# Twelve matmuls ahead of all else, decay rows padded to 128, thirty more fills and a new order in a fused mixer kernel

## The chip, the cores and the metric

The kernel runs as one program on one core of a Trainium2 chip. The metric is the device time of one execution in microseconds (us), as the median of the runs. A profile holds one execution; its span goes from the first to the last instruction. Engines are named as the profile names them: PE (TensorE matmuls), PEld (its weight loads), DVE (VectorE), ACT (ScalarE), POOL (GpSimd), SP (SyncE, which issues most DMAs).

## What is computed

Three layers follow one another, for 4 batches, 8 heads, 768 steps and head size 40 (model width 320):

```python
def _attn_ref(q, k, v, i_gate, f_gate, o_gate):
    ...
    for t in range(S):
        m_new = np.maximum(f_gate[:, :, t] + m, i_gate[:, :, t])
        f_stab = np.exp(f_gate[:, :, t] + m - m_new)
        i_stab = np.exp(i_gate[:, :, t] - m_new)
        m = m_new
        C = f_stab[:, :, None, None] * C + i_stab[:, :, None, None] * np.einsum('bhd,bhe->bhde', vt, kt)
        n = f_stab[:, :, None] * n + i_stab[:, :, None] * kt
        ...
        y[:, :, t] = o * h_tilde / denom

def _moe_ref(x, w_val, conv_w, w_out):      # causal convolution of 5 taps as a gate
    ...
    val = x @ w_val
    return (gate * val @ w_out).astype(np.float32)

def _moe2_ref(x, w_ch1, w_ch2):             # Fourier mixing, layer norm, two-layer perceptron
    X = np.fft.fft(np.fft.fft(x, axis=1), axis=2)
    u = x + np.real(X).astype(np.float32)
    ...
    ch = np.maximum(un @ w_ch1, 0.0) @ w_ch2
    return (u + ch).astype(np.float32)
```

## The kernel before

**Attention.** The recurrence is cut into chunks of 128 steps, six for each batch, and each chunk into two halves of 64 steps. For a chunk the decay of each head is spread over 128 partitions by matmuls into a PSUM bank (`a_fb`), and DVE scans that bank into `d` (`a_pre`). For the first four chunks of batch 0 `a_fb` uses 16 small matmuls of 32 rows (the profile's `bank<-f,pat`). For all 20 other chunks it is one matmul of 24 rows and 512 columns, `bank<-gsp,sel`: `gsp` holds the decay rows of the four batches, 24 rows for each, at partitions 0, 32, 64 and 96 of one buffer; `sel` is a constant that picks rows. Then come `bank<-qk` (40 rows), `bank<-kvo` and `bank<-kvo,d` (64 rows, 41 columns), `bank<-cc,e` (40 rows) and, for batch 0, `bank<-eg,epat` (32 rows). None of these uses all 128 rows of the array. Each float32 matmul of the program stands in the profile as two instructions.

**Gate and mixing.** The output of a chunk is transposed (`bank<-pat,x`), three chunks make a half of a batch, and on it run the convolution (`xT,dg` on PE for three of the pieces, DVE for the rest), the value product (`xH,wvH` and seven like it), the output product (`woH,gH` and so on), the Fourier steps (`cs,eo`, `dmat,w`), a layer norm and the perceptron (`uu,w1H` ... and `w2H,hh` ...). These use all 128 rows. The weights come as 64-bit floats, are taken apart by DVE and ACT (`raw` to `mk`) and split into high and low parts.

**What sets the order.** Every operation is recorded as a unit in a list (`_Plan`), and `emit` replays the units in the order of the table `ORDER`, written out by hand or by a search outside the kernel; `CELL` says which buffer or PSUM bank each tile gets. So every engine's queue is fixed by `ORDER`. The table `FILLS` inserts extra matmuls before a unit: `(n, m, k)` puts m products of a constant 128x128 tile into bank k before unit n; nobody reads their result. In the profile they are `bank<-pat` of L343, and there are 42. All recorded instructions have one line, L292, so that tile names tell them apart.

The steps that the change touches are `fill` (L341 to L344), `prologue_pads` (L389), `prologue_spread` (L436), which loads `gsp` once for all batches, `prologue_const` (L450), which loads `sel`, `a_fb` (L577), and the replay `emit` (L279). The first operations on PE are two transposes of the input gate, which wait for the constant `pat`.

Of the kernel before, what the change touches and what calls it, by code (L numbers as in the profile page):

```python
# [33 lines left out]
NQK = 2  # L34
FB0 = 4
# [131 lines left out]
]  # L167
FILLS = [
    (25, 1, 3), (207, 4, 6), (199, 5, 6), (219, 2, 4), (426, 2, 1), (460, 2, 0), (488, 4, 1), (515, 15, 3), (575, 5,
    3), (1023, 2, 1),  # L170
]

# [83 lines left out]
class _Plan:  # L256
# [7 lines left out]
    def add(self, eng, method, a, k):  # L264
# [9 lines left out]
        for x in sorted(ins, key=lambda x: x.t is out):  # L274
            if not x.t.n:
                self.tiles.append(x.t)
                x.t.n = len(self.tiles)

    def emit(self):  # L279
        held = [t for t in self.tiles if t.kind is not None]  # L280
        for t, n in zip(held, CELL, strict=True):
            t.cell = n
# [896 lines left out]
```

## Time and profile before

| | us |
|---|---|
| median of 3 runs (502.08 to 503.85) | 502.46 |
| the profiled execution, its own time | 502.64 |
| its span | 500.8 |
| PE busy in the span | 470.4 (94%) |
| PEld busy | 428.5 (86%) |
| DVE busy | 336.9 (67%) |
| ACT busy | 179.2 (36%) |
| POOL busy | 152.7 (30%) |

Around the span lie 1.84 us. In the chain of work that ended last PE has 69% and DVE 17%. The rows are read so: a row of the timeline has the start in us from the start of the span, the length of the group, the engine, the line, the operation, out<-in, the form (partitions x elements), and the number of instructions; in brackets stands idle time of the engine before it and what ended it. The step of a group, from its start to the start of the next, tells better than its length what it costs, since matmuls overlap. The column PEclk is the granted clock of TensorE as a share of its upper level: 1.00 is 2.4 GHz and 0.50 is 1.2 GHz.

### The profile page before, as it was taken

How to read it: one execution, taken by the hardware profiler on the slowest of the kernel's cores; microseconds unless marked ns; L12 is line 12 of the kernel's file. 1: busy time of each engine (PE TensorE's matmuls, PEld its weight loads, DVE VectorE, ACT ScalarE, POOL GpSimd, SP SyncE). 2: the span in 40 equal slices, each digit the busy share in tenths (PEclk: the TensorE clock that was granted, in tenths of full speed). 3: DMA queues.
4: the chain of work that ended last, by engine and by line, in shares of the span. 5: the costliest groups of instructions: out<-in, count | busy, mean ns of one | idle time of the engine just before them, and what ended most of it. 6: DMA issues, size and time to landing. Idle time of an engine off the chain costs nothing.

```text
span 500.8 us, 13774 instructions
## 1 busy us (share of the span) xinstructions
PE 470.4 (94%) x5728; PEld 428.5 (86%) x5728; DVE 336.9 (67%) x812; ACT 179.2 (36%) x407; POOL 152.7 (30%) x204
## 2 busy tenths in 40 slices
PE   4999989789999999989999999989999999999997
PEld 4988877678989989878898899878998898999997
DVE  8565878799866758688557677586677584762321
ACT  4244455346314325335133354143243342341110
POOL 1434443433653250414432414114425212010000
PEclk9999899999999999999999999999999999999999
DMA  7623557356312144200332205002210010000100
GB/s 231 207 88 105 146 171 230 112 167 187 108 50 80 41 130 120 55 29 5 89 97 82 64 15 199 14 1 68 86 58 15 3 41 1 1 13 1 41 27 26
DMA packets 23397, 40.16 MB, mean 80 GB/s; under 512 B 4744, under 2 KB 14280, under 8 KB 23336
## 3 DMA queue, kind: packets, MB, share of 16 engines
q1 hardware_dynamic: 23192, 38.90, 25.5%
q8 instruction: 45, 0.74, 0.6%
q0 software_dynamic: 144, 0.39, 0.2%
q14 instruction: 16, 0.13, 0.1%
HBM read 33.09 MB, written 4.23 MB: 75 GB/s over the span
## 4 chain that ended last, share of the span: by engine, by line
PE 69%; DVE 17%; issue 5%; ACT 4%; DMA 2%; POOL 2%; POOLq 0%; ACTq 0%; SPq 0%; DVEq 0%
PE bank L292 68%; DVE bank L292 2%; DVE z L292 2%; DVE bs L292 2%; DVE hl L292 1%; PE bank L343 1%; DVE t L292 1%; DMA raw<-in_w_dram 1%; DVE uu L292 1%; DVE mk L292 1%; DVE d L292 1%; POOL r L292 1%; DMA pat<-in_c_pat_dram 1%; ACT xH L292 1%; DVE xL L292 1%
## 5 line engine op out<-in xcount | busy, mean ns | idle before, releaser
L292 PE MATMUL bank<-uu,w1H 128*128 128x256 f32 x480 | 94.8, 289 | 1.8 <-DVE uu L292 0.9
L292 PEld LDWEIGHTS bank<-uu,w1H 128*128 128x128 f32 x480 | 74.3, 190 | 6.1 <-issue 1.9
L292 PE MATMUL bank<-w2H,hh 128*128 128x320 f32 x240 | 75.6, 322 | 0.0
L292 PE MATMUL bank<-w2L,hh 128*128 128x320 f32 x240 | 72.4, 309 | 0.0
L292 DVE SCALAR_TENSOR_TENSOR hl<-bank,hh 128x512 fp32r<-128x512 f32 x60 | 41.1, 687 | 42.0 <-ACT hh L292 41.7
L292 PE MATMUL bank<-uu,w1L 128*128 128x256 f32 x240 | 67.7, 282 | 0.0
L292 ACT ACTIVATE hh<-bank 128x512 fp32r<-128x512 f32 x60 | 35.7, 597 | 75.7 <-PE bank L292 75.7
L292 PE MATMUL bank<-w2H,hl 128*128 128x320 f32 x240 | 55.0, 310 | 1.6 <-DVE hl L292 1.6
L292 DVE SCALAR_TENSOR_TENSOR bank<-xT,cw,bank 128x384 f32<-128x384 f32 x84 | 48.6, 618 | 0.6
L292 PEld LDWEIGHTS bank<-w2H,hh 128*128 128x128 f32 x240 | 45.1, 188 | 1.9 <-issue 1.4
L292 PEld LDWEIGHTS bank<-uu,w1L 128*128 128x128 f32 x240 | 45.6, 190 | 0.0
L292 PEld LDWEIGHTS bank<-w2L,hh 128*128 128x128 f32 x240 | 45.2, 188 | 0.2 <-POOL w2L L292 0.2
L292 PEld LDWEIGHTS bank<-w2H,hl 128*128 128x128 f32 x240 | 40.0, 188 | 2.4 <-DVE hl L292 2.4
L292 PE MATMUL bank<-uu,w1T 128*128 128x256 f32 x120 | 34.2, 285 | 0.1
L292 PE MATMUL bank<-uu,w1U 128*128 128x256 f32 x120 | 33.7, 281 | 0.0
L292 DVE TENSOR_TENSOR z<-z,bank 128x161 f32<-128x161 f32 (+2 forms) x72 | 25.3, 370 | 12.0 <-PE bank L292 11.5
L292 POOL TENSOR_TENSOR cc<-cc,fcol 128x164 f32<-128x164 f32 x40 | 19.8, 495 | 43.6 <-DVE cc L292 25.5
L292 DVE TENSOR_TENSOR_SCAN d<-bank,pat 128x512 f32<-128x512 f32 x24 | 29.2, 1216 | 5.0 <-PE bank L292 4.9
L292 POOL TENSOR_TENSOR gL<-gg,gH 128x384 fp32r<-128x384 f32 x16 | 16.2, 1021 | 51.4 <-ACT gH L292 40.4
L292 DVE TENSOR_TENSOR d<-bank,d 128x512 f32<-128x512 f32 x24 | 16.6, 690 | 19.3 <-PE bank L292 15.8
L292 POOL TENSOR_TENSOR kvo<-kvo,r 128x320 f32<-128x320 f32 x24 | 18.3, 762 | 34.7 <-DVE r L292 29.2
L292 POOL TENSOR_TENSOR kvo<-kvo,d 128x320 f32<-128x320 f32 x24 | 17.8, 742 | 34.5 <-DVE d L292 21.3
(146 smaller groups left out, 1039.0 us busy)
## 6 DMA issues: line engine op xcount, KB each, us to landing
kvo<-in_kvo_dram SPq DMA_DIRECT2D x24, 484.0 KB
qk<-in_qk_dram SPq DMA_DIRECT2D x48, 160.0 KB
raw<-in_w_dram SPq DMA_DIRECT2D x9, 640.0 KB
out_dram<-z SPq DMA_DIRECT2D x24, 160.0 KB
e<-sce SPq DMA_DIRECT2D x30, 80.0 KB
cs<-in_c_cs_dram SPq DMA_DIRECT2D x2, 386.0 KB
raw<-in_w_val_dram SPq DMA_DIRECT2D x1, 640.0 KB
raw<-in_w_out_dram SPq DMA_DIRECT2D x1, 640.0 KB
```

What stands on the lines that cost most here:

```text
L292: getattr(engine, method)(*a, **k)
L343: nc.tensor.matmul(out=banks()[:, k, 0:L], lhsT=a, rhs=a, start=True, stop=True)
```

## The change

The code around the tables:

```diff
+WARM = 12
...
     def emit(self):
+        self.warm()
         held = [t for t in self.tiles if t.kind is not None]
...
     def fill(n, k):
-        a = pat.real()[:, 0:L]
+        a = ones.real()
         for _ in range(n):
             nc.tensor.matmul(out=banks()[:, k, 0:L], lhsT=a, rhs=a, start=True, stop=True)
 
+    def warm():
+        a = ones.real()
+        nc.vector.memset(a, 1.0)
+        for _ in range(WARM):
+            nc.tensor.matmul(out=banks()[:, 7, 0:L], lhsT=a, rhs=a, start=True, stop=True)
...
-    gsp = ct("gsp", [128, H * LS], F32R)
+    gsps = [ct("gsp%d" % n, [128, H * LS], F32R) for n in range(2)]
...
+        for t, n in ((gsps[0], 4), (sel, 6), (gsps[1], 4)):
+            A.activation(t.rearrange("p (a n) -> p a n", n=L), ones.unsqueeze(1).to_broadcast([128, n, L]), AF.Copy,
+                         scale=0.0)
+
+    def gate_rows(b):
+        SP.dma_start(out=f(gsps[b % 2][0:24]),
+                     in_=scr[:, :, b * H:b * H + H].rearrange("n g h t -> (n g) (h t)"))
...
-        for b in range(B):
-            r = 32 * ((b - 1) % B)
-            SP.dma_start(out=f(gsp[r:r + 24]),
-                         in_=scr[:, :, b * H:b * H + H].rearrange("n g h t -> (n g) (h t)"))
...
-        G.dma_start(out=sel, in_=c_sel)
+        G.dma_start(out=sel[0:24], in_=c_sel)
...
-            r = slice(32 * ((b - 1) % B), 32 * ((b - 1) % B) + 24)
-            g = gsp[r].rearrange("r (h t) -> r h t", h=H)
-            T.matmul(out=fb, lhsT=sel[r, L * c:L * c + L], rhs=g, start=True, stop=True)
+            g = gsps[b % 2].rearrange("r (h t) -> r h t", h=H)
+            T.matmul(out=fb, lhsT=sel[:, L * c:L * c + L], rhs=g, start=True, stop=True)
...
+                if n == 0:
+                    run("rows", gate_rows, b)
```

The fills are now products of a tile of ones, there are 72 of them in place of 42, and `ORDER` and `CELL` are new throughout (their first lines stand for all):

```diff
 FILLS = [
-    (25, 1, 3), (207, 4, 6), (199, 5, 6), (219, 2, 4), (426, 2, 1), (460, 2, 0), (488, 4, 1), (515, 15, 3), (575, 5,
-    3), (1023, 2, 1),
+    (39, 4, 1), (71, 3, 1), (44, 3, 3), (86, 2, 0), (90, 1, 0), (207, 1, 3), (214, 9, 6), (221, 5, 6), (426, 4,
+    1), (467, 3, 1), (474, 6, 0), (511, 26, 3), (585, 3, 2), (937, 1, 1), (1835, 1, 0),
 ]
 ORDER = [
-    0, 3, 4, 1, 5, 2, 54, 6, 8, 9, 74, 10, 7, 76, 53, 11, 75, 12, 16, 13, 17, 27, 14, 115, 20, 15, 28, 67, 32, 29, 33,
+    3, 0, 4, 12, 5, 7, 8, 251, 13, 1, 9, 6, 57, 49, 2, 11, 114, 10, 75, 14, 19, 103, 74, 30, 20, 15, 31, 23, 35, 25,
...
```

A branch of `a_fin` that was never taken is deleted as well. Counted by kind, DVE gets one instruction more (the memset of the ones), ACT three (the zeros of the two buffers and of `sel`), PE 42 (12 + 30); all others are the same in number and form.

PE, the start of the program (names: `pat,gi` transposes the input gate, `f,pat` spreads decays, `fm,epat` and `eg,epat` spread sums of decays). Before:

```order
L292 MATMUL bank<-pat,gi 128x32 x2
L292 MATMUL bank<-f_87,pat 64x64 x16
L292 MATMUL bank<-pat,gi 128x32 x4
L343 MATMUL bank<-pat 128x128
L292 MATMUL bank<-fm,epat 128x64
L292 MATMUL bank<-f_87,pat 64x64 x16
L292 MATMUL bank<-fm,epat 128x128
```

and after:

```order
L351 MATMUL bank<-ones 128x128 x12
L294 MATMUL bank<-pat,gi 128x32 x2
L345 MATMUL bank<-ones 128x128 x4
L294 MATMUL bank<-pat,gi 128x32 x4
L345 MATMUL bank<-ones 128x128 x3
L294 MATMUL bank<-eg,epat 128x128 x4
L294 MATMUL bank<-fm,epat 128x64
L345 MATMUL bank<-ones 128x128 x3
L294 MATMUL bank<-fm,epat 128x128
L294 MATMUL bank<-f_99,pat 64x64 x16
```

The twelve products of ones stand ahead of the first transposes, ten fills stand between the products of the gates, and the decays of the first chunk come behind them.

PE, where the decays of the fifth and sixth chunk of batch 0 are spread. Before, the sixth chunk's:

```order
L292 MATMUL bank<-qk_70 64x64 x16
L292 MATMUL bank<-kvo,d 64x41 x16
L292 MATMUL bank<-gsp,sel 128x512
L343 MATMUL bank<-pat 128x128 x5
L292 MATMUL bank<-eg,epat 128x128 x4
L292 MATMUL bank<-pat,x 128x128 x3
L292 MATMUL bank<-kvo 64x41 x16
```

and after, the fifth chunk's:

```order
L294 MATMUL bank<-qk_83 64x64 x16
L294 MATMUL bank<-kvo,d 64x41 x16
L294 MATMUL bank<-kvo 64x41 x16
L294 MATMUL bank<-pat,x 128x128 x3
L294 MATMUL bank<-gsp_87,sel 128x512
L345 MATMUL bank<-ones 128x128 x9
L294 MATMUL bank<-pat,x 128x128 x3
```

The second transpose of batch 0 now stands ahead of the first `gsp` product, and nine fills behind it where five stood behind the second one.

PE, one of the `gsp` products of batch 1, within the perceptron of batch 0. Before:

```order
L292 MATMUL bank<-uu,w1T 128x256
L292 MATMUL bank<-uu,w1U 128x256
L292 MATMUL bank<-gsp,sel 128x512
L292 MATMUL bank<-xH,wvH 128x384
L292 MATMUL bank<-xH,wvL 128x384
```

and after:

```order
L294 MATMUL bank<-w2L,hh 128x320
L294 MATMUL bank<-w2H,hl 128x320 x2
L294 MATMUL bank<-gsp_104,sel 128x512
L294 MATMUL bank<-w2H,hh 128x320
L294 MATMUL bank<-w2L,hh 128x320
```

The product still stands between products of 128 rows, and now has 128 rows itself. Its columns (512) are unchanged.

## Rows read from the trace of the kernel before

**Rows 1.** Windows: stretch, length, busy (count) PE, PEld, DVE, ACT, POOL, PEclk, DMA, GB/s.

```profile
0.00:6.63 6.63, 0.00 (x0) 0.03 (x1) 4.97 (x12) 2.04 (x3) 1.92 (x7) 1.00 0.64 212
6.63:48.55 41.92, 41.48 (x637) 36.50 (x637) 26.49 (x59) 15.75 (x44) 14.54 (x22) 1.00 0.51 155
48.55:55.37 6.82, 6.64 (x117) 4.64 (x115) 6.62 (x14) 3.39 (x9) 2.84 (x5) 1.00 0.30 75
55.37:58.79 3.42, 3.42 (x12) 3.19 (x12) 2.66 (x7) 2.11 (x7) 0.26 (x1) 0.50 0.51 126
58.79:112.83 54.04, 47.48 (x491) 38.55 (x489) 45.63 (x119) 25.22 (x57) 24.10 (x26) 1.00 0.57 174
112.83:497.31 384.48, 371.37 (x4478) 345.57 (x4478) 250.02 (x606) 130.70 (x291) 109.01 (x145) 1.00 0.19 56
```

**Rows 2.** Timeline of PE, 15 to 49 us, chosen rows.

```profile
15.11 1.97 PE L292 MATMUL bank<-f,pat 32*64 32x64 f32 x32
...
39.05 1.09 PE L292 MATMUL bank<-kvo,d 64*64 64x41 f32 x32 [0.16 <-issue]
...
40.79 2.50 PE L343 MATMUL bank<-pat 128*128 128x128 f32 x10
43.22 2.07 PE L292 MATMUL bank<-eg,epat 32*128 32x128 f32 x8
45.22 0.90 PE L292 MATMUL bank<-pat,x 128*128 128x128 f32 x3
...
48.59 3.46 PE L292 MATMUL bank<-xT,dg 128*128 128x384 f32 x10
```

**Rows 3.** Timeline of PE, the same forms later.

```profile
53.62 0.68 PE L292 MATMUL bank<-kvo,d 64*64 64x41 f32 x32
54.22 1.15 PE L292 MATMUL bank<-eg,epat 32*128 32x128 f32 x8
...
74.41 3.49 PE L292 MATMUL bank<-xT,dg 128*128 128x384 f32 x10
...
79.14 0.34 PE L292 MATMUL bank<-xH,wvH 128*128 128x384 f32 x1
79.32 0.34 PE L292 MATMUL bank<-xH,wvL 128*128 128x384 f32 x1
...
110.67 1.28 PE L343 MATMUL bank<-pat 128*128 128x128 f32 x10
```

**Rows 4.** Timeline of PE: its first row, and the first chunk's last product.

```profile
6.63 0.39 PE L292 MATMUL bank<-pat,gi 32*128 32x32 f32 x2 [6.63 <-DMA pat<-in_c_pat_dram]
...
23.04 1.09 PE L292 MATMUL bank<-kvo,d 64*64 64x41 f32 x32
```

**Rows 5.** Timeline of DVE: the product that this last one needs.

```profile
19.16 0.69 DVE L292 TENSOR_TENSOR d<-bank,d 128x512 f32<-128x512 f32 x1 [0.74 <-PE bank L292]
```

**Rows 6.** Timeline of ACT, 3 to 12 us.

```profile
3.32 1.28 ACT L292 ACT_TABLE_LOAD   x1 [3.32 <-DMA gi<-in_ig_dram]
4.93 0.42 ACT L292 ACTIVATE gi<-gi 32x256 f32<-32x256 f32 x1 [0.33 <-DVE gi L292]
...
11.01 0.83 ACT L292 ACTIVATE fh<-f 32x768 fp32r<-32x768 f32 x1
```

**Rows 7.** Timeline of PE around one `gsp` product of batch 1.

```profile
138.46 0.28 PE L292 MATMUL bank<-uu,w1T 128*128 128x256 f32 x1
138.57 0.28 PE L292 MATMUL bank<-uu,w1U 128*128 128x256 f32 x1
138.78 0.49 PE L292 MATMUL bank<-gsp,sel 24*128 24x512 f32 x1
139.21 0.42 PE L292 MATMUL bank<-w2H,hh 128*128 128x320 f32 x1
```

**Rows 8.** Timeline of PEld, the weight loads of the last two.

```profile
138.78 0.18 PEld L292 LDWEIGHTS bank<-gsp,sel 24*128 24x128 f32 x1
139.20 0.19 PEld L292 LDWEIGHTS bank<-w2H,hh 128*128 128x128 f32 x1 [0.24 <-issue]
```

More of the change, by code (lines that the diff above doesn't have):

```diff
@@ L340, in fill @@
     def fill(n, k):
-        a = pat.real()[:, 0:L]
+        a = ones.real()
         for _ in range(n):
             nc.tensor.matmul(out=banks()[:, k, 0:L], lhsT=a, rhs=a, start=True, stop=True)
+    def warm():
[3 more added lines that the diff above has]
+            nc.tensor.matmul(out=banks()[:, 7, 0:L], lhsT=a, rhs=a, start=True, stop=True)
     plan.fill = fill
+    plan.warm = warm
     pat = ct("pat", [128, L + 512])
     ident, ipat = pat[:, 0:L], pat[:, L:]
+    ones = ct("ones", [128, L])
     epat = ct("epat", [32, 5 * L + 16])
     sel = ct("sel", [128, S], F32R)
-    gsp = ct("gsp", [128, H * LS], F32R)
+    gsps = [ct("gsp%d" % n, [128, H * LS], F32R) for n in range(2)]
     cs = [ct("cs%d" % t, [128, 4, NQ]) for t in range(2)]
@@ L702, in a_fin @@
         r = wt("r", [128, H], "r")
+        o = t["o"]
         A.activation(r.rearrange("q (p s) -> q s p", s=2), pv[:, :, :, D], AF.Abs)
-        o = t["o"]
-        if RD:
-            V.tensor_scalar(r, r, 1.0, None, op0=ALU.max)
-            G.tensor_tensor(h8(o), h8(o), r.unsqueeze(2).to_broadcast([128, H, D]), op=ALU.divide)
-        else:
-            V.tensor_scalar(r, r, 1.0, None, op0=ALU.max)
-            V.reciprocal(r, r)
-            G.tensor_tensor(h8(o), h8(o), r.unsqueeze(2).to_broadcast([128, H, D]), op=ALU.mult)
+        V.tensor_scalar(r, r, 1.0, None, op0=ALU.max)
+        V.reciprocal(r, r)
+        G.tensor_tensor(h8(o), h8(o), r.unsqueeze(2).to_broadcast([128, H, D]), op=ALU.mult)
         x = wt("x", [128, DM], "C")
@@ L1013, in m_out @@
         ml.pop((b, i))
-    XL, ES, LN, WLO, XT, CA, EV, RD, WM = V, (V, V, V, V), (V, V, V, V), G, (), (), (), 0, V
+    XL, ES, LN, WLO, XT, CA, EV, WM = V, (V, V, V, V), (V, V, V, V), G, (), (), (), V
     def run(what, fn, *a):
@@ L1086, in _constants @@
     c["c_ep"] = np.concatenate(ep, 1).astype(np.float32)
-    sel = np.zeros((4, 32, S), np.float32)
-    sel[:, 0:24] = np.tile(np.repeat(np.eye(NG), LS, 1), (2, 1))
-    c["c_sel"] = sel.reshape(128, S)
+    c["c_sel"] = np.tile(np.repeat(np.eye(NG), LS, 1), (2, 1)).astype(np.float32)
     n = np.arange(Q)
```

248 rows, old and new, of tables (CELL, ORDER) are left out of this document.

## The prediction

> **What bounds the kernel now.** I read the page first: PE is busy for 94% of the span and has 69% of the chain that ended last. Then the windows by stretch [rows 1], to see where PE is the bound and at which clock. From 112.83 to 497.31 us PE is busy for 371.37 of 384.48, and DVE for 250.02: PE bounds that stage, and 13.1 us are left in it to idle. From 58.79 to 112.83 PE (47.48 of 54.04) and DVE (45.63, 84%) wait for each other, since the weights are taken apart on DVE there. From 6.63 to 48.55 PE is busy for 41.48 of 41.92, DVE for only 26.49.
>
> The last of these is not what it seems. PEclk reads 1.00 there, and the durations contradict it. The same group of `kvo,d` takes 1.09 at 39.05 and 0.68 at 53.62, `eg,epat` 2.07 and 1.15, ten instructions of a fill 2.50 and 1.28 [rows 2, 3]. The convolution at 48.59 takes 3.46 and at 74.41 3.49, so that the upper level holds from about 48.6 us. The stretch from 55.37 to 58.79, which the column does give as 0.50 (1.2 GHz), has the same look: 12 matmuls in 3.42 us, where steps of 0.18 are usual later [rows 1, 3]. I go by the durations: PE ran at the lower level until 48.6 us, although it hardly idled, and fell back for 3.4 us after a run of narrow products (40 and 64 rows, then the 32 rows of `eg,epat`). Wide work (128 rows), the convolution or the value products, stood ahead of both the upper stretches.
>
> The Trainium skill ("TensorE: Matmul & The Clock Gate", "Why this matters for your kernels") advises to keep TensorE continuously busy and free of long idle gaps, and its clock stays up. The trace does not agree: 41.48 of 41.92 us busy, at the lower level.
>
> **The change, part by part.** The profiled execution took 502.64 us, 0.18 above the median of 502.46; I sum against 502.6.
>
> *Warm-up and the first ten fills.* PE sat idle for 6.63 us until `pat` came [rows 4]. Twelve products at the lower level cost 12 x 0.49 = 5.9 us (five fills step 2.43, 40.79 to 43.22 [rows 2]), so they lie within that wait. They are the widest work there is, and I expect the clock at its upper level by 5 to 8 us. `pat` now comes behind the first `kvo` load instead of a `qk` load; the warm-up covers what that costs, and if it did not, it would be a microsecond at most. The ten fills behind it (0.25 each at the upper level) stand where PE waits for the scalar chain of DVE and ACT, and cost nothing as long as that chain is late; without the cover they cost 2.5 us.
>
> *Zeros.* Three operations on ACT, of 512, 768 and 512 columns: by 0.83 for 768 [rows 6] about 0.55 + 0.83 + 0.55 = 1.9 us behind the table load (1.28). ACT idled for 3.32 us at the start and began its first exponential at 4.93 [rows 6], so this ends a few tenths ahead of it. The memset of ones on DVE has 128 columns, under 0.2 us by 0.69 for 512 [rows 5]. Together 0; if the cover were gone, 0.5.
>
> *The rows' loads.* They now come once for each batch (48 KB), two early and two in the batches before they are needed, and wait on SP for earlier loads, not for PE; nothing queues behind them that is late. The load of `sel` moves behind six POOL products, and PE wants it only at the fifth chunk. 0.
>
> *First part, up to the first value product (55.30 us before).* A held clock would be worth much: narrow groups cost 0.57 to 0.62 of their time [rows 2, 3], so PE's 41.5 us would be some 24. But DVE then bounds: it has 4.97 + 26.49 + 6.62 = 38.1 us up to 55.37 [rows 1], and in the next stage, at the upper level, it reached 84%; 38.1 / 0.84 = 45 to 46 us. So 10 us is the most that I give this part. For the clock, however, the new order has no wide work between the tenth fill and the nine fills at the fifth chunk, but three single fills and two transposes; in between stand the narrow products that the clock fell behind at 55.37, and PE will idle among them as well. I expect a fall at about 16 to 18 us. Then: `kvo,d` of the first chunk waited for a product that DVE began at 19.16, and itself ran at 23.04 [rows 4, 5]; now it can run at about 18.5 to 19, DVE's list ahead of it being the same work. From there to the nine fills the new order has 10 groups at about 1.0 (`kvo,d`, `kvo`, `qk`, `cc,e`), three `eg,epat` at 2.0, an `f,pat` at 1.9, two transposes at 0.8 and a fill: 20 us at the lower level [rows 2], 11 at the upper one. So the nine fills start at about 39, 4.5 us at the lower level; in them the clock comes back, say they end at 42.5. Then 8.3 us at the upper level: transposes 0.3, three narrow groups 1.6, five convolution products (ten instructions) 3.2, `eg,epat` 1.1, `gsp` 0.24, `kvo` 0.65, five fills 1.2. First value product at 51, or 46 with the clock held; the first microseconds of the run should still be at the upper level, and I take 50: a gain of 5.3.
>
> *The second slow stretch* goes in either case, since the nine fills are followed by the convolution, five fills and 24 value products, all wide. Its 12 wide products, 3.42 us, need half: a gain of 1.6 (bounds 0 and 1.7).
>
> *Later fills.* 44 stand behind the first value product, 30 did before: 14 x 0.25 = 3.5 us more. In 58.79 to 112.83 PE idled for 6.6 us [rows 1]. I take 0; the bound is 3.5 lost.
>
> *Padding.* A `gsp` product of 512 columns steps 0.43 (138.78 to 139.21), and the product ahead of it steps 0.21 where its like takes 0.11 [rows 7]. A wide one of 384 columns steps 0.18 [rows 3], so 512 wide columns should take 0.24. The reason is in the loads: that of `gsp` begins with its product at 138.78, and the next begins only at 139.20 [rows 8], each in the open. Padded, I expect both hidden, as between other wide products. That is 0.19 + 0.09 = 0.28 for the 12 of the 18 products of batches 1 to 3 that have wide neighbours on both sides, and about 0.18 for the other 6: 3.4 + 1.1 = 4.5 us. PE being the bound there to 97%, I take 4.0 (bounds 0 and 4.5).
>
> The Trainium skill ("TensorE: Matmul & The Clock Gate", Part 3, "The mechanism") says that weight loads overlap matmuls in flight only when the row group differs. By that rule a product on all rows would keep its loads in the open and the gain here would be nothing (rival three). The rows so far speak against it: the narrow load, in its own row group, is the one in the open.
>
> **Sum.** 502.6 - 5.3 - 1.6 - 4.0 = 491.7 us. Its own range is 488 to 497: one microsecond of a later or earlier return of the clock is about half a microsecond of time, and the bounds above do the rest.
>
> **Rivals.**
>
> 1. *The clock holds.* For it: the fills and warm-up raise what PE does. By the Trainium skill's advice named above it would hold too. Against it: the fall at 55.37 behind work of the same kind. The first part gains 10 instead of 5.3: 502.6 - 10 - 1.6 - 4.0 = 487.0.
> 2. *Slower: fills without a clock.* If the clock falls at once behind the warm-up and the nine fills do not lift it, or it falls again within the convolution, 28 fills stand ahead of the first value product where 12 did, each 0.49 on an engine that hardly idles: 16 x 0.49 = 7.8. With the padding's gain: 502.6 + 7.8 - 4.0 = 506.4. It decides from the point where the value products start later than 55.3. Against it: a shorter row of wide work than nine fills and a product raised the clock by 48.6.
> 3. *Padding does nothing*, by the rule above or since the extra time belongs to the 512 columns: 495.7.
> 4. *The new order loses later.* All of it is new, and an order doesn't show how long a wait is. If PE's idle time after the first part grows from 13.1 to about 22, what was won goes: 491.7 + 9 = 500.7. For it: DVE, already at 84% in the middle stage, gets its weight work pressed into less time. Against it: PE's list there is the same work.
>
> **Chances.** The forecast 0.47, the held clock 0.28, slower 0.06, padding without effect 0.05, a later loss 0.10, better than all of these 0.04. The range 482.5 to 500.0 holds all but the last, the slower case and most of the later loss. A measurement of this kernel can tell about 0.5% (2.5 us) from no change. Faster by more: 0.47 + 0.28 + 0.05 + 0.04 and a little of the later loss, 0.86; within: 0.08; slower: 0.06.
>
> **What would show it.** The durations of `kvo,d` and `eg,epat` by 10, 20 and 35 us (1.09 and 2.07, or 0.68 and 1.15) tell the clock, whatever PEclk prints; PEclk should now have entries before 48 us. The first value product should stand at 50 (46 if the clock holds). A `gsp` step should be 0.24 and the one ahead of it as its like. No PEclk of 0.50 should stand behind the nine fills. I am wrong if the value products start after 54, if the `gsp` step stays at 0.43, or if PE's idle time in the stage of batches 1 to 3 is over 20 us.

## The result

The kernel after takes 489.86 us in the median of four runs (489.58 to 490.25), the kernel before 503.04 beside it (502.08 to 503.85). The ratio is 0.9736 with a 95% interval of 0.9719 to 0.9754: 13.2 us less. The prediction was 491.7, in a range of 482.5 to 500.0. The number holds. The way to it does not: the first part, from which 5.3 us were to come, became longer, and more than that came from a place that was taken as 0.

The windows of the kernel after, cut where its granted clock changes (columns as in [rows 1]):

```profile
0.00:6.32 6.32, 5.26 (x24) 5.19 (x24) 4.75 (x11) 3.58 (x5) 1.50 (x7) 1.00 0.70 206
6.32:13.15 6.83, 6.30 (x70) 5.34 (x70) 6.11 (x14) 5.91 (x14) 0.51 (x1) 1.00 0.96 273
13.15:47.28 34.13, 32.77 (x588) 29.47 (x584) 18.55 (x44) 8.70 (x26) 13.10 (x21) 0.50 0.54 150
47.28:57.76 10.48, 9.98 (x170) 7.41 (x169) 9.03 (x20) 4.83 (x12) 5.38 (x7) 1.00 0.36 107
```

The clock rises at 6.32, within the warm-up, falls at 13.15 and comes back at 47.28; from there to the end no entry of 0.50 follows. (Ahead of the first entry the column prints 1.00 even where the durations show the lower level, as in [rows 1, 2]; a mean clock counts that time as the upper level too.) The next three lines are the same kernel by stage: up to the first value product, up to the first `uu,w1H`, and to the last product. Under them stand the first part and the middle stage of the kernel before, which [rows 1] cut at its clock; its last stage is the last line of [rows 1].

```profile
0.00:57.76 57.76, 54.31 (x840) 47.40 (x840) 38.44 (x87) 23.02 (x57) 20.48 (x34) 0.70 0.58 163
57.76:111.97 54.21, 49.92 (x464) 42.58 (x465) 49.03 (x120) 27.51 (x64) 24.56 (x25) 1.00 0.50 143
111.97:484.80 372.83, 366.42 (x4509) 345.26 (x4509) 247.79 (x607) 130.02 (x291) 109.58 (x146) 1.00 0.20 60
```

```profile
0.00:55.30 55.30, 48.05 (x751) 41.10 (x751) 38.01 (x82) 21.11 (x54) 19.30 (x33) 1.00 0.50 152
55.30:112.83 57.53, 50.98 (x501) 41.81 (x500) 48.36 (x125) 27.39 (x63) 24.36 (x26) 0.97 0.56 171
```

The first part is 2.5 us longer (55.30 to 57.76), the middle stage 3.3 shorter (57.53 to 54.21), the stage of PE 11.65 shorter (384.48 in [rows 1] to 372.83): 12.5 in all, which is the difference of the two spans (500.8 and 488.3). In the last stage PE is busy for 5.0 us less and idle for 6.7 less (13.1 to 6.4). The stages do not hold quite the same work: of the middle stage's narrow groups the new order has put one `kvo` group (about 0.6 us) into the first part and one `qk` group into the last, and one `gsp` product has come from the last stage into the middle.

Timeline of PE in the kernel after, chosen rows of the first part:

```profile
14.50 1.25 PE L294 MATMUL bank<-qk 40*64 40x64 f32 x32 [0.97 <-DMA qk<-in_qk_dram]
15.68 3.67 PE L294 MATMUL bank<-f,pat 32*64 32x64 f32 x64
...
24.27 1.09 PE L294 MATMUL bank<-kvo,d 64*64 64x41 f32 x32
...
37.21 2.07 PE L294 MATMUL bank<-eg,epat 32*128 32x128 f32 x8
...
44.49 0.78 PE L294 MATMUL bank<-gsp,sel 128*128 128x512 f32 x1
45.06 3.23 PE L345 MATMUL bank<-ones 128*128 128x128 f32 x18
...
57.76 0.44 PE L294 MATMUL bank<-xH,wvH 128*128 128x384 f32 x1 [0.36 <-DVE e L294]
...
60.65 0.34 PE L294 MATMUL bank<-xH,wvH 128*128 128x384 f32 x1
```

The last row is the seventeenth value product. In the kernel before, sixteen ran from 55.30 to the group of its row 59.90:

```profile
59.90 1.15 PE L292 MATMUL bank<-eg,epat 32*128 32x128 f32 x8
```

`kvo,d` of the first chunk runs at 24.27, later than the 23.04 of [rows 4]; its 1.09 and the 2.07 of `eg,epat` are the durations of the lower level in [rows 2]. And around one `gsp` product of batch 1, PE first and then the weight loads, answering [rows 7, 8]:

```profile
139.04 0.46 PE L294 MATMUL bank<-w2H,hl 128*128 128x320 f32 x2
139.34 0.39 PE L294 MATMUL bank<-gsp,sel 128*128 128x512 f32 x1
139.56 0.31 PE L294 MATMUL bank<-w2H,hh 128*128 128x320 f32 x1
```

```profile
139.20 0.19 PEld L294 LDWEIGHTS bank<-gsp,sel 128*128 128x128 f32 x1
139.34 0.19 PEld L294 LDWEIGHTS bank<-w2H,hh 128*128 128x128 f32 x1
```

The `gsp` product steps 0.22 where it stepped 0.43, and the two products ahead of it step 0.30, 0.15 each, as `w2H,hh` does (139.56 to 139.71 in the same timeline). The load of `gsp` begins at 139.20, ahead of its product, and the next one's at 139.34, with it. Of the 17 `gsp` products of the last stage seven step 0.23 like this one, the others 0.31 to 0.44.

### The profile page after: what moved, and what is told of

Its sections match the earlier page's. It is cut to its first block, busy times and chain, and to the rows that moved or that the text cites. A ratio compares the mean times of both kernels' runs of the same rounds, so it can differ in the third digit from the quotient of the medians.

```text
span 488.3 us, 13902 instructions
## 1 busy us (share of the span) xinstructions
PE 470.6 (96%) x5812; PEld 435.2 (89%) x5812; DVE 335.8 (69%) x813; ACT 180.6 (37%) x410; POOL 154.6 (32%) x204
## 4 chain that ended last, share of the span: by engine, by line
PE 75%; DVE 13%; issue 5%; DMA 3%; ACT 2%; POOL 1%; SPq 0%; ACTq 0%; DVEq 0%; POOLq 0%
PE bank L294 74%; DVE z L294 2%; DMA qk<-in_qk_dram 2%; DVE bs L294 1%; DVE w L294 1%; DVE mk L294 1%; PE bank L345 1%; DVE bank L294 1%; DVE uu L294 1%; DVE t L294 1%; DMA pat<-in_c_pat_dram 1%; DMA raw<-in_w_dram 1%; DVE hl L294 1%; DVE r L294 1%; ACT od L294 0%
## 5 line engine op out<-in xcount | busy, mean ns | idle before, releaser
L294 PE MATMUL bank<-w2H,hh 128*128 128x320 f32 x240 | 74.5, 318 | 0.1
L294 POOL TENSOR_TENSOR r<-ve,mhalf 128x2 f32<-128x2 f32 x12 | 8.8, 736 | 78.0 <-DVE ve L294 78.0
L294 DVE TENSOR_TENSOR z<-z,bank 128x159 f32<-128x159 f32 (+2 forms) x72 | 25.3, 371 | 10.9 <-PE bank L294 10.4
```

Of the source, the lines that this page charges most:

```text
L294: getattr(engine, method)(*a, **k)
```

## The experiments

Each kernel ran beside the kernel before on its chip; a time is the median of four runs, and what is compared between chips is the ratio to the kernel before. The stages are those of one profiled execution of each:

| kernel | median (runs), us | ratio, 95% interval | first value product at | middle stage | last stage (PE idle in it) |
|---|---|---|---|---|---|
| before | 503.04 (502.08 to 503.85) | 1 | 55.30 | 57.5 | 384.5 (13.1) |
| after | 489.86 (489.58 to 490.25) | 0.9736, 0.9719 to 0.9754 | 57.76 | 54.2 | 372.8 (6.4) |
| again | 490.73 (489.61 to 491.79) | 0.9751, 0.9732 to 0.9770 | 57.69 | 53.8 | 373.2 (6.7) |
| narrow | 494.28 (493.11 to 495.60) | 0.9811, 0.9779 to 0.9842 | 58.85 | 54.4 | 376.0 (5.6) |
| padonly | 499.66 (499.56 to 500.21) | 0.9921, 0.9902 to 0.9940 | 55.50 | 58.2 | 381.2 (14.1) |
| nowarm | 493.05 (491.55 to 495.72) | 0.9793, 0.9756 to 0.9831 | 58.65 | 53.8 | 374.7 (8.1) |
| nonine | 492.51 (491.83 to 492.84) | 0.9775, 0.9756 to 0.9795 | 60.55 | 53.6 | 373.0 (6.4) |
| nolate | 493.50 (487.55 to 493.60) | 0.9778, 0.9723 to 0.9832 | 52.01 | 54.4 | 375.8 (7.4) |
| hold_fills | 487.23, 488.74 and 509.14, 509.21 | 0.9697, 0.9677 to 0.9717, of the first two | 73.25 | 54.7 | 375.9 (7.7) |
| hold_rows | 480.56 (480.43 to 481.41) | 0.9555, 0.9539 to 0.9571 | 47.64 | 54.1 | 373.3 (7.4) |
| rows_alone | 479.05 (478.32 to 481.88) | 0.9542, 0.9504 to 0.9580 | 46.76 | 53.9 | 372.2 (6.7) |
| rows_nowarm | 483.97 (483.40 to 488.69) | 0.9656, 0.9595 to 0.9717 | 50.62 | 54.1 | 374.1 (7.0) |
| early_qk | 489.10 (488.16 to 490.76) | 0.9700, 0.9656 to 0.9744 | 55.51 | 54.2 | 373.1 (6.8) |
| rows_early | 481.41 (480.41 to 481.89) | 0.9538, 0.9491 to 0.9584 | 47.71 | 54.1 | 374.5 (7.1) |

Run again is the kernel after, unchanged, as the base of the runs beside it:

> The kernel after unchanged, beside the others on the same chip, as their base: 489 to 491, the first value product at 57 to 59 us, the later stage 372 to 374 us with 5 to 8 us of waits.

It came out inside every one of these bands.

### The padding, undone and alone

Run narrow undoes one thing in the kernel after:

```diff
-            g = gsps[b % 2].rearrange("r (h t) -> r h t", h=H)
-            T.matmul(out=fb, lhsT=sel[:, L * c:L * c + L], rhs=g, start=True, stop=True)
+            g = gsps[b % 2][0:24].rearrange("r (h t) -> r h t", h=H)
+            T.matmul(out=fb, lhsT=sel[0:24, L * c:L * c + L], rhs=g, start=True, stop=True)
```

> The kernel after with one thing undone: the 18 decay products read 24 rows of the two buffers instead of 128. Theory A (the gain of 13 us is some 4.3 us from the padding, 1.6 us from the second slow stretch and some 7 us from fewer waits of TensorE in the later stage, nothing from the first part): a gsp product between wide neighbours goes from 0.23 back to 0.43 us and the one ahead of it from 0.14 to 0.2, the time rises by 3.5 to 4.6 us, to 493.5 to 494.5. Theory B (the gain comes from the clock and the order alone, the padding is covered by other waits): the rows grow the same, the time stays at 490 within 1 us.

Run padonly puts the padding alone into the kernel before, with its fills and its order but for one unit (the load of the last batch's rows comes later). Left out of the cut are the zeros (four memsets, two on DVE and two on POOL) and the constant `sel`, now of 24 rows:

```diff
-    gsp = ct("gsp", [128, H * LS], F32R)
+    gsps = [ct("gsp%d" % n, [128, H * LS], F32R) for n in range(3)]
...
-            SP.dma_start(out=f(gsp[r:r + 24]),
+            SP.dma_start(out=f(gsps[b % 3][0:24]),
...
-            T.matmul(out=fb, lhsT=sel[r, L * c:L * c + L], rhs=g, start=True, stop=True)
+            T.matmul(out=fb, lhsT=sel[:, L * c:L * c + L], rhs=g, start=True, stop=True)
```

> The kernel before, its order, its fills and its clock as they were, with the padding alone: the four batches' decay rows in three zeroed buffers of 128 rows (the load of the last batch's rows is issued later, when the first buffer is free). Theory A: 503.0 falls by 3.5 to 4.6 us, to 498.4 to 499.5, and the clock's rise and fall near 48 to 59 us stay where they were. Theory B: 503 within 1 us, the saved time turns into waits on other engines.

The last stage of both, in windows (narrow first), then the `gsp` product of narrow that answers the one above:

```profile
113.27:489.31 376.04, 370.42 (x4509) 345.25 (x4509) 248.16 (x607) 129.81 (x291) 109.86 (x146) 1.00 0.20 60
```

```profile
113.68:494.86 381.18, 367.05 (x4478) 345.08 (x4478) 249.51 (x606) 130.20 (x291) 109.04 (x145) 1.00 0.19 57
```

```profile
140.44 0.45 PE L294 MATMUL bank<-w2H,hl 128*128 128x320 f32 x2
140.83 0.49 PE L294 MATMUL bank<-gsp,sel 24*128 24x512 f32 x1
141.25 0.41 PE L294 MATMUL bank<-w2H,hh 128*128 128x320 f32 x1
```

With 24 rows the step is 0.42 again, and the two ahead of it take 0.39 instead of 0.30. PE is busy for 370.42 instead of 366.42 (4.0 more); in the other direction 367.05 instead of 371.37 (4.3 less). About one microsecond of that turns into waits: the stage changes by 3.2 and 3.3 us. By the ratios the time changes by 3.0 to 3.8 (0.9811 against 0.9751 and 0.9736, of 503.5) and by 4.0 (0.9921). For narrow the stage is the better measure, since its first part is 1.1 us longer as well, with its clock back at 48.86 instead of 47.28; whether the padding has a part in that is not shown. In size theory A holds in both, at the lower edge of its band for narrow, and theory B in neither; the padding is worth about the same in either order.

These two runs also separate the order. Narrow has the products of the kernel before in their old form, nearly the same busy time (370.42 and 371.37; the `qk` group more and the `gsp` product less about cancel), and 8.4 us less in the last stage. So the new order, with the new cells, is worth 8.4 us there, 7.5 of it PE's idle time (13.1 to 5.6). The waits of PE in that stage, before and then after, longest sums (engine, what waited, for whom: us in total, times, longest):

```profile
PE bank L292 <- ACT un L292: 2.5, 4, 0.9
PE bank L292 <- DVE hl L292: 2.1, 5, 1.0
PE bank L292 <- DVE uu L292: 1.6, 2, 0.9
PE bank L292 <- DVE xL L292: 1.0, 2, 0.5
```

```profile
PE bank L294 <- ACT un L294: 1.3, 3, 0.6
...
PE bank L294 <- DVE hl L294: 0.7, 2, 0.5
PE bank L294 <- DVE uu L294: 0.7, 3, 0.3
```

The gain is not one wait: the four lines of before (the normalised rows `un`, `uu`, the low parts `hl` and `xL`) are 7.2 us in 13 waits, the first three of them after are 2.7 in 8, and `xL` is no longer among the waits listed. DVE and ACT have nearly the same work in the stage (250.0 and 247.8, 130.7 and 130.0 us), so it was moved, not saved. Which of the moves did it was not tried.

In one point padonly missed theory A, which wanted the clock's rise and fall where they were. In its profiled execution the clock rose at 49.32 and had no second fall, and yet its middle stage is no shorter than before (58.2 and 57.5). Timeline of PE in padonly:

```profile
56.66 0.34 PE L296 MATMUL bank<-xH,wvT 128*128 128x384 f32 x1
57.95 0.41 PE L296 MATMUL bank<-xH,wvU 128*128 128x384 f32 x1 [0.96 <-DMA wvU<-tl]
```

At the upper level the value products reach `wvU` before its load has landed, and wait 0.96 us. From the first value product to the `eg,epat` behind the first two groups it is 4.2 us here (55.50 to 59.70), against 4.6 in the kernel before (55.30 to 59.90), which ran most of them at the lower level. The kernel after starts them 2.3 us later and doesn't meet this wait: there the same sixteen take 2.9 (57.76 to 60.65).

### The first part: warm-ups and fills taken away

```diff
-WARM = 12
+WARM = 0
...
-    (39, 4, 1), (71, 3, 1), (44, 3, 3), (86, 2, 0),
+    (86, 2, 0),
```

> The kernel after without the twelve warm-ups and without the ten fills that stand in the first 21 us. Theory A (the first part gains nothing from its clock): the granted clock stays at the lower level until the nine fills at about 45 us, the first value product comes at 56 to 59 us (57.8 with them), the time stays at 488.5 to 491.5. Theory B (the warm-ups and the early fills carry a part of the gain): the first value product comes at 61 or later and the time is 493 or more.

The clock rises only at 48.02, and yet the first value product comes at 58.65, 0.9 us later than with the warm-ups. By the ratios the time is 2.1 (against 0.9751) to 2.9 us (against 0.9736) above the kernel after; the interval is clear of after's, not of again's. Theory A is right on the first part, but 493.05 us is over its band; that is theory B's time, while B's mark, a first value product at 61 or later, isn't met. In the profiled execution most of the rest lies in the last stage (374.7 instead of 372.8), where one wait of PE for `un`, at 125.0, is 1.8 us instead of 0.6, and ACT had waited ahead of it (its timeline):

```profile
122.03 0.78 ACT L291 ACTIVATE mk<-raw 128x640 f32<-128x640 f32 x1 [1.86 <-DMA raw<-in_w_dram]
```

The runs of nowarm spread over 4 us. Why that load of a weight block is late here stays open.

Run nonine takes the other fills of the first part:

```diff
-(207, 1, 3), (214, 9, 6), (221, 5, 6),
+(207, 1, 3),
```

> The kernel after without the nine fills behind the first gsp product and without the five fills ahead of the first value products; warm-ups and early fills stay. Theory A (the nine fills are what brings the clock back): the clock comes back only in the conv products or in the value products, 52 us or later, the first value product comes at 59 to 63 us, the time is 493 to 498. Rival: the conv products alone bring the clock back before the value products, the 3 us of the fills are saved, the first value product comes at 57 or earlier and the time is 488 to 490.

The clock comes back at 55.34, behind the convolution's products, instead of 47.28. The first value product comes at 60.55 and the time is 492.51, just under the band of theory A: the nine fills do bring the clock back, and together with the five are worth 1.2 to 2.0 us by the ratios, with the 4.6 us that they take already paid (the interval is clear of after's, not of again's).

Run early_qk moves one load to an earlier place, so that the wait of 0.97 us at 13.5 goes:

```diff
-..., 114, 10, 75, 14, ..., 21, 76, 56, 18, 55, ...
+..., 114, 10, 56, 75, 14, ..., 21, 76, 18, 55, ...
```

> The kernel after with one load moved: the second half of the first chunk's q and k is issued right behind the decay constants (place 19 of the order instead of 40), so that TensorE need not wait for it at 13.5 us. Theory A (the two waits of about 1 us in the first 15 us are what lets the clock fall early): without that wait the clock holds beyond 20 us, the first value product comes at 51 to 54 and the time is 483.5 to 486.5, as in the profiled execution of the run without late fills. Theory B (the narrow products let it fall, wait or no wait): the fall stays at 10 to 14 us, the first value product at 56.5 to 58.5, the time is 488.5 to 491.

The wait is gone and the clock falls at 13.31 all the same: theory B. The mean clocks of its four runs, 0.962 to 0.968, fit an early fall in each. `kvo,d` runs at 22.94 and the first value product at 55.51, 2.2 us earlier and a microsecond ahead of B's band. By the ratios the time gains 1.8 to 2.6 us (0.9700 against 0.9736 and 0.9751), but the intervals overlap, so this gain isn't shown; 489.1 lies in the band of theory B.

### The later fills, and a second course of the same first part

Run nolate leaves out the 44 fills behind the first value product, (426, 4, 1) to (1835, 1, 0), and nothing else.

> The kernel after without the 44 fills that stand behind the first value product, 26 of them in one place near 103 us. Theory A (they lie in waits of TensorE and the products around them keep the clock): the clock stays at the upper level, the later stage keeps its 373 us, the time is within 1.5 us of the kernel after. Rival (they carry the clock over the narrow places at 60 to 110 us): the clock falls for 3.4 us or more there and the time rises by 2 to 5 us.

Three runs took 493.46 to 493.60, one, the profiled one, 487.55. Its windows by clock:

```profile
7.25:24.32 17.07, 14.93 (x330) 13.09 (x330) 11.88 (x25) 6.73 (x18) 5.99 (x9) 1.00 0.74 203
24.32:41.38 17.06, 16.71 (x315) 15.10 (x316) 11.52 (x34) 7.50 (x22) 7.38 (x12) 0.50 0.69 191
...
99.41:109.65 10.24, 4.78 (x19) 4.07 (x20) 9.94 (x34) 4.26 (x9) 4.38 (x5) 0.50 0.75 234
...
130.13:133.54 3.41, 3.41 (x16) 3.41 (x16) 1.25 (x3) 1.05 (x3) 2.24 (x3) 0.50 0.72 241
```

```profile
104.08 1.54 PE L291 MATMUL bank<-pat,un 128*128 128x128 f32 x6 [6.93 <-ACT un L291]
```

Two results. Without the 26 fills PE idles for 6.9 us at 97.1, waiting for `un` (timeline of PE, the row above), and the clock falls for 10.24 us and once more for 3.41: the rival's mechanism. The last stage is 375.8 instead of 372.8, and the three other runs lie 2.8 us over again's median. So the later fills earn about 3 us, most of them in a wait where they cost nothing. The ratio of the four runs doesn't show it (its interval, 0.9723 to 0.9832, takes in again's 0.9751), since the profiled run gained more than that in its first part.

The other result was not looked for. The first part of this program is that of the kernel after, instruction by instruction, and here the clock rose at 7.25 and held until 24.32, not until 13.15. Timeline of PE:

```profile
14.03 2.08 PE L291 MATMUL bank<-f,pat 32*64 32x64 f32 x64
...
19.02 0.68 PE L291 MATMUL bank<-kvo,d 64*64 64x41 f32 x32
...
24.41 1.28 PE L291 MATMUL bank<-cc,e 40*64 40x41 f32 x29 [1.94 <-DVE e L291]
...
38.88 0.78 PE L291 MATMUL bank<-gsp,sel 128*128 128x512 f32 x1
39.45 3.10 PE L342 MATMUL bank<-ones 128*128 128x128 f32 x18
...
52.01 0.45 PE L291 MATMUL bank<-xH,wvH 128*128 128x384 f32 x1 [0.36 <-DVE e L291]
```

These are the moments of the prediction nearly to the microsecond: `kvo,d` forecast for 18.5 to 19 and here at 19.02, the nine fills for 39 and here at 39.45, the first value product for 50 to 51 and here at 52.01. In part that is chance: the fall was forecast for 16 to 18 and came at 24.32, and what the clock gave in between went into a wait of 1.94 us. The mean clocks say that the course is rare: 0.968 in this run, 0.951 to 0.954 in the other three, which is 45 to 48 us at the lower level instead of 31. In the eight runs of the kernel after and again the mean was 0.961 to 0.967, 32 to 38 us at the lower level, which fits an early fall in each. Narrow and nonine, whose first part is the same up to there, fell at 11.31 and 10.97. What decides between the courses stays open; early_qk speaks against the wait for `qk`.

### Holding the clock

Run hold_fills spreads more fills over the narrow stretch (40; the 36 of the expectation is a miscount), and leaves three of the nine:

```diff
-(214, 9, 6)
+(67, 3, 6), (84, 3, 6), (77, 3, 6), (106, 3, 6), (81, 2, 6), (175, 2, 6), (110, 2, 6), (180, 4, 6), (214, 3, 6)
...
```

> The kernel after with 36 more fills spread over the narrow stretch (two to four ahead of a group of narrow products, in a bank that nothing else uses there) and with three instead of nine behind the first gsp product. Theory A (the prediction's rival of the clock that holds): the granted clock stays at the upper level from about 6 us on, gsp comes at 38 to 41 us instead of 44.5, the first value product at 50 to 53, the time falls by 4 to 8 us against the kernel after, to 482 to 486. Rival 1 (the chain over VectorE bounds the stretch as soon as TensorE is faster): the clock holds, but the first value product comes at 55 or later and the time is within 2 us of the kernel after. Rival 2 (too few wide columns): the clock falls again before 30 us and the added fills cost 4 us or more.

Two courses again: 487.23 and 488.74 us in two runs, with a mean clock of 1.0 and 0.996, and 509.14 and 509.21 in the other two, with 0.953 and 0.945. The profiled one is of the second kind. Its windows:

```profile
6.14:9.55 3.41, 2.37 (x19) 1.94 (x19) 2.78 (x8) 1.81 (x5) 0.00 (x0) 1.00 0.99 260
9.55:53.93 44.38, 44.13 (x513) 38.96 (x513) 14.78 (x34) 7.55 (x22) 10.13 (x16) 0.50 0.39 109
```

PE is busy for 2.37 of 3.41 us behind the rise, the clock falls at 9.55, and the added fills then stand in the way, each at twice its price, for 44.38 us, 44.13 of them busy, without bringing it back: rival 2 in these two runs. In the two others the clock held and the time fell by 2.0 to 3.5 us against again, less than theory A's 4 to 8. No profile shows these two; that the fills used up a good part of what the clock gave (34 more of them at 0.25 us are 8.5, by estimate) is argued, not shown.

Run hold_rows gets wide work without added instructions. The products that spread the gates (`f,pat` and `eg,epat`) are made over 128 rows instead of 32, the 96 added rows zero:

```diff
-    f0 = wt("f0", [32, S], "M")
-    eg = wt("eg", [32, S], "M")
+    f0w = wt("f0", [128, S], "M")
+    egw = wt("eg", [128, S], "M")
+    f0, eg = f0w[0:32], egw[0:32]
...
-                    T.matmul(out=fb[64 * x:64 * x + 64, h, :], lhsT=ident[0:32, h:h + 1].to_broadcast([32, LS]),
-                             rhs=f0[:, LS * g:LS * g + LS], start=True, stop=True)
+                    T.matmul(out=fb[64 * x:64 * x + 64, h, :], lhsT=ident[:, h:h + 1].to_broadcast([128, LS]),
+                             rhs=f0w[:, LS * g:LS * g + LS], start=True, stop=True)
...
-                T.matmul(out=ep[:, p], lhsT=epat[:, p * L:(p + 1) * L], rhs=eg[:, c * L:(c + 1) * L], start=True, stop=True)
+                T.matmul(out=ep[:, p], lhsT=epw[:, p * L:(p + 1) * L], rhs=egw[:, c * L:(c + 1) * L], start=True, stop=True)
```

The zeros are six memsets on POOL. The constant `epat` gets 128 rows as well (`epw`), and `eg` stands in another cell. Twelve fills are added in the gaps, and four stand in place of the nine.

> The kernel after with the narrow products of the gates' spread (f,pat and eg,epat) made over 128 rows instead of 32, the added 96 rows zero, 12 more fills in the gaps between them, and four instead of nine behind the first gsp product. Theory A (zero rows are work for the clock as other rows are): the clock stays at the upper level from about 6 us on with a third of the added fills, the first value product comes at 47 to 52 us, the time is 480 to 486. Rival 1 (zeros, or rows, do not count): the clock falls near 13 us as in the kernel after, the first value product comes at 57 or later, the time is 489 to 493. Rival 2 (VectorE bounds the stretch): the clock holds, the first value product at 55 or later, the time within 2 us of the kernel after.

Run rows_alone has the same wide rows and the fills of the kernel after, none added:

> The kernel after with the products of the gates' spread over 128 rows as in the run with rows and fills (96 zero rows added), and with after's own fills, none added. Theory A (the rows themselves hold the clock): the clock stays at the upper level from 5 to 7 us on or falls once for a short time, the first value product comes at 45 to 49 us, the time is 478 to 483. Theory B (the twelve added fills are needed): the clock falls before 30 us in some or all executions, the first value product comes at 52 to 58 in such an execution, the time is 485 to 491 and spread by more than 2 us.

Windows of rows_alone, up to the clock's rise, to the first value product, and the last stage:

```profile
0.00:3.96 3.96, 2.91 (x13) 2.91 (x14) 2.46 (x7) 3.16 (x4) 3.23 (x10) 1.00 0.50 133
3.96:46.76 42.80, 37.23 (x829) 31.28 (x827) 35.35 (x81) 19.58 (x53) 21.66 (x31) 1.00 0.75 207
...
100.70:472.92 372.22, 365.55 (x4509) 344.22 (x4509) 247.53 (x607) 129.86 (x291) 109.60 (x146) 1.00 0.20 60
```

Theory A in both. The clock rises at 3.96, a little ahead of the band (4.76 in hold_rows), and has no entry of 0.50 until the last products are done; the first value product comes at 46.76 and 47.64, 10 to 11 us earlier than in the kernel after, and the rest of the time is unchanged. Rows_alone is at 0.9542 of the kernel before, by the ratios 9.8 to 10.5 us under the kernel after, and not to be told from hold_rows (0.9555); the twelve added fills aren't needed (theory B of rows_alone falls), though one of its four runs took 481.88 with a mean clock of 0.989.

Run rows_nowarm is hold_rows without the warm-ups and the first ten fills, as in nowarm.

> The kernel with 128 rows and twelve added fills, without the twelve warm-ups and without the ten fills of the first 21 us. Theory A (once the rows are full, the products themselves raise the clock, and the warm-ups are worth little): the clock rises by 20 us and holds, the first value product comes at 48 to 51 us, the time is 480.5 to 484. Theory B (the clock has to be up before the narrow stretch begins, or it stays down until the wide products): the clock rises at 25 us or later, the first value product comes at 53 or later, the time is 486 or more.

The clock rises at 18.89, the first value product comes at 50.62, the time is 483.97: in the bands of theory A, but not "little", 3.0 us in the first part and 5 by the ratios. With rows that hold the clock the warm-ups and early fills earn more in the first part than the 0.9 us of the kernel after.

Run rows_early joins the wide rows and the earlier load of early_qk.

> The two best edits together: products of the gates' spread over 128 rows (none of the added fills), and the q and k load issued earlier. Theory A (the early load takes away a wait on the path to the first value product): 477 to 479 in all executions, the first value product at 45 to 46.5 us. Theory B (the load is not on that path, VectorE is): 478.5 to 480, as with the rows alone. If the earlier load pushes others back, the first chunk's kvo among them, the time is 480 to 482.

It is no faster than the rows alone (0.9538 and 0.9542). Theory A falls: 481.41 us is over its band and the first value product came at 47.71. The time is that of the third case, in which the earlier load pushes others back, and the profiled execution shows such a load (timeline of DVE, then of ACT):

```profile
23.20 0.17 DVE L296 TENSOR_SCALAR mk<-mk 128x15 f32<-128x15 f32 x1 [2.52 <-ACT mk L296]
```

```profile
22.95 0.22 ACT L296 ACTIVATE mk<-raw 128x15 f32<-128x15 f32 x1 [5.32 <-DMA raw<-in_conv_w_dram]
```

The convolution's weights, 15 numbers to a row, land at 22.9. ACT waits 5.32 us for them, DVE behind it 2.52, and the product `e` that stands on DVE behind that is what PE then lacks (1.65 us at 22.4). `kvo,d` of the first chunk had run at 18.95, 1.3 us ahead of rows_alone; that gain goes here. Behind this wait the clock falls, from 26.29 to 33.11, and the mean clocks of the four runs, 0.989 to 0.993, are 7 to 11 us at the lower level in each. The same small load was the 1.94 us at 22.5 in nolate. In rows_alone it lands at 21.1 and PE doesn't wait for it. What differs is the issue on SP of its last piece, 19.81 here and 17.79 there; ACT starts on it 3.1 and 3.3 us later. A version with this load ahead of the others was not tried.

## Why the prediction was right, and where it was not

**Warm-up, zeros, loads.** Right. The clock was at its upper level at 6.32 (forecast 5 to 8), and nothing waited for the zeros or the rows' loads.

**The first part, -5.3 us.** Wrong: +2.5. The step that failed is the moment of the fall, "at about 16 to 18 us". It fell at 13.15, and the list up to `kvo,d` ran at the lower level: `f,pat` 3.67 instead of the 2.08 that it takes in nolate, the rest likewise, and 0.97 of waiting for `qk`. That makes the 24.27 where 18.5 to 19 was forecast. From there the working holds: 20.8 us to the nine fills (forecast 20), 3.1 for them (3.5), the clock back in them, and 9.6 to the first value product (8.3). Of the 7.8 us between 57.76 and the forecast 50, some 5.3 are the late `kvo,d`, 1.7 the steps behind it, and 0.8 is what the working took off at its end for a start at the upper level. The prediction had put a mark for this itself: value products later than 54 mean that it is wrong. They came at 57.76, later even than before, which is the point from which its slower rival decides; that rival's price was not reached, since the clock did come back.

What the prediction could not have read from one trace is that the moment of the fall is not a property of the program. The same first part gave 13.15 in the profiled execution of the kernel after, 13.01 in again's and 24.32 in nolate's, and with the last of these the first value product came at 52.01. Even this course, which one run in the twelve of these three kernels took, gave 3.3 of the 5.3 us (55.30 to 52.01).

**The held clock, rival one.** Not what happened in the kernel after, but its estimate fits what happened where the clock held: the working bounded a first part with a held clock by DVE, 38.1 us of work at 84%, 45 to 46 us. Rows_alone has the clock, 37.8 us of DVE work up to the first value product (2.46 + 35.35), and 46.76.

**The second slow stretch, -1.6.** Right in mechanism and size: the stretch is gone, and the sixteen value products take 2.9 us (57.76 to 60.65) instead of 4.6 (55.30 to 59.90), a gain of 1.7. It could have been less: padonly gained 0.4 us from the same change of the clock, since it came to `wvU` before that had landed. The other half of the middle stage's 3.3 us was not forecast: two narrow groups moved out of the stage, and PE's idle time in it went from 6.6 to 4.3.

**Later fills, 0.** They did no harm that shows. The 14 more than before were not tried by themselves; all 44 are worth about 3 us (nolate), because 26 of them stand in a wait of 7 us in which the clock would fall.

**Padding, -4.0.** Right in mechanism and size: step 0.22 (forecast 0.24), the ones ahead 0.15 as their like, both loads hidden; 4.0 to 4.3 us of PE's busy time, 3.2 to 3.3 of the stage, 3.0 to 4.0 of the time. Rival three, with the rule of the Trainium skill that it leans on ("TensorE: Matmul & The Clock Gate", Part 3, "The mechanism"), falls: the load of 128 rows for `gsp` began at 139.20 under the product ahead, and it is the one of 24 rows that was in the open.

**The later order, 0.** The largest miss: -8.4 us in the last stage (narrow against before). The prediction saw the 13.1 us of idle time and asked only whether it might grow (rival four); for its shrinking it had no term, and at most the 0.04 of "better than all of these". There was a reason to ask: idle time of PE in a stage that PE bounds to 97%, with DVE at 65% and ACT at 34%, in some two dozen waits of at most a microsecond, is what an order can remove, and this one removed 7.5 of the 13.1 us.

In sum: forecast -5.3 for the first part, -1.6 for the slow stretch, -4.0 for the padding and 0 for the later order; found +2.5, -1.7 (and -1.6 more in the middle stage), -3.2 and -8.4. That the total came out within 2 us is luck: the first part's miss of 7.8 and the order's of 8.4 have opposite signs.

## What to carry to other kernels

To keep the clock, try first to make the narrow products themselves wide with zero rows, where their instructions don't take longer for it, as here; filler that works only while the clock is up costs double when it falls. A program near the edge has more than one course; read the clock of several executions before a term is hung on the moment at which it falls. And idle time of the bounding engine, spread over many short waits, is a term of its own in any change of order, with a size between 0 and all of it.

## What the runs showed of the hardware

Rows of zeros were enough to hold the clock: with 96 of 128 rows of `f,pat` and `eg,epat` zero it held from 3.96 us to the last products (rows_alone), where with 32 rows it fell at 13.15. It is no guarantee: in rows_early, with the same rows, it fell at 26.29 behind a wait of 1.65 us. The zero rows cost no time on PE: 64 instructions of `f,pat` took 2.08 us at the upper level with 32 rows (nolate, above) and the same with 128 (timeline of PE in hold_rows):

```profile
15.52 2.08 PE L293 MATMUL bank<-f,pat 128*64 128x64 f32 x64
```

The length of the first upper stretch behind the same warm-up was 3.41 us (hold_fills), 6.83 (after, again) or 17.07 (nolate), by execution and by what followed, and the rise itself came anywhere from 3.96 (rows_alone) to 7.25 us (nolate) after the start. And taking away a wait of 0.97 us at 13.5 (early_qk) didn't move the fall (13.31).
